# Second feed-forward product with the weights stationary and 448 tokens moving, its sums and the output transposed, the residual rebuilt on GpSimd

## The chip, the cores and the metric

The kernel runs on one core of a Trainium2 chip. The metric is the device time of one execution in microseconds (us). A core has TensorE (PE: matmuls; its weight loads are shown apart as PEld), VectorE (DVE), ScalarE (ACT), GpSimd (POOL) and SyncE (SP, which issues most of the DMAs). TensorE multiplies a stationary operand of 128 × 128 with a moving operand of up to 512 columns and adds the result up in PSUM, of which there are eight banks of 512 columns.

## What is computed

```python
x = attention(q, k, v)                 # 4 batches, 12 heads, 448 tokens, 64 each; causal softmax
x = x.transpose(0, 2, 1, 3).reshape(4, 448, 768)
gate = sigmoid(causal_conv5(x, conv_w))
x = (gate * (x @ w_val)) @ w_out       # 768 x 768 each
mu, var = mean(x), mean((x - mu) ** 2) # per token
xn = (x - mu) / sqrt(var + 1e-6) * g_ln
out = x + relu(xn @ w_ch1) @ w_ch2     # 768 -> 3072 -> 768; the kernel before sums x + ... in acc
```

## The kernel before

The kernel has three stages. The first does attention, convolution and gate, and the value product, batch by batch; its matmuls for the value product stand in line 517, and its output, feature by token, goes to DRAM (`y_dram`). The second, the norm stage, takes the 1,792 tokens as 14 tiles of 128: it loads a tile (`yl`, line 619), multiplies it with `w_out` (line 635, 36 matmuls of 384 columns), takes mean and variance from the result in PSUM, scales it (ScalarE, line 669), transposes it with six matmuls (line 677) and leaves the normed tile, feature by token, as a high and a low part (`xnh`, `xnl`). ScalarE also copies the sum itself to `acc[t]` (line 652), tokens in the partitions, as the residual.

The third stage is the feed-forward. Every float32 product is made of three matmuls: high × high, high × low, low × high. The 24 blocks of 128 hidden features are taken in 12 groups of two (`G = 2`), and the tokens in four steps of 256, 512, 512 and 512 (`TM`). For one group and step, `ch1` does the first product (`ch1_products`, line 586): the weights are stationary, the tokens move, and for each of the two blocks 18 matmuls are summed in one bank (six pieces of the 768 features times three parts). ScalarE applies relu and rounds (`hh`, line 747), VectorE makes the low part (`hl`, line 748). `ch2` does the second product (line 761): for each tile of 128 tokens `hh` and `hl` are stationary, and half a row of `w_ch2`, 384 columns, moves; six matmuls are summed, and VectorE adds the result to `acc[t]` (line 766). In the last group the finished tiles are stored.

The order of the third stage is written out: `ch1` runs two steps ahead of `ch2`, and behind each `ch2` some steps of the preparation of the next group's weights are issued (`advance`): VectorE turns the raw words of a block into float32 (lines 207 to 227), ScalarE rounds it (line 200), VectorE takes the low part (line 243). The order of the first two stages comes from a planner (`Plan`), which places tasks by due times and assumed costs. The first product of the first step, `ch1_products(0, 0, j)`, is one of its tasks and fills TensorE while the last tile is normed.

The outputs of the first product lie in three banks (`ps_1`) and, for the small step, in one (`ps_e`); those of the second in four (`ps_2`).

Of the kernel before, what the change touches and what calls it, by code (L numbers as in the profile page):

```python
# [145 lines left out]
def f32(ap):  # L146
    return ap.bitcast(F32)
# [3 lines left out]
def attention_gate_ffn(  # L151
# [12 lines left out]
    nc = tc.nc  # L164
    B, NP, P = qk.shape[:3]
    H, S = 2 * NP, out.shape[1]
# [10 lines left out]
    NEG_SCALE = -1.0 / float(D) ** 0.5  # L177
    ot = out.rearrange("b s d -> (b s) d")

# [11 lines left out]

    g_t = const.tile([P, KC], F32, name="g_t")
    y_dram = [dram.tile([DM, S], F32, name=f"y_dram{b}") for b in range(B)]

# [51 lines left out]
    with ExitStack() as ph1:  # L246
# [40 lines left out]
        task = plan.task  # L287
# [244 lines left out]

    accp = ctx.enter_context(tc.tile_pool(name="accp", bufs=1, reuse_waits="tile"))
    acc = [accp.tile([P, DM], F32, name=f"acc{t}") for t in range(NTILE)]
    G = 2
    TB = 4 * P
    TM = [list(range(NTILE % 4))] + [list(range(t, t + 4)) for t in range(NTILE % 4, NTILE, 4)]
    NM = len(TM)
    NG = NJ // G
    with ExitStack() as ph2:  # L540
        ff = ph2.enter_context(tc.tile_pool(name="ff", bufs=1, reuse_waits="tile"))
        xnh = ff.tile([P, KC, NT], F32R, name="xnh")
        xnl = ff.tile([P, KC, NT], F32R, name="xnl")
        w_t = {}

# [22 lines left out]

        ps_e = ph2.enter_context(tc.tile_pool(name="ps_e", bufs=1, space=PSUM))
        ps1_t = {}  # L570

        def ch1_products(g, m, j):
            lo, hi = TM[m][0] * P, (TM[m][-1] + 1) * P
            if m > 0:
                ps1_t[g, m, j] = ps_1.tile([P, 1, TB], F32, tag="a", name="ps1")
                ps = ps1_t[g, m, j][:, 0]
            else:
                if j == 0:
                    ps1_t[g] = ps_e.tile([P, G, hi - lo], F32, tag="e", name="ps1")
                ps1_t[g, m, j] = ps1_t[g]  # L580
                ps = ps1_t[g][:, j]
# [11 lines left out]
        with ExitStack() as ph2a, tc.manual_schedule():  # L593
# [6 lines left out]
                "yl": (yr_p, [P, KC, P], F32R, 3), "yh": (yr_p, [P, KC, P], F32R, 2),  # L600
                "st": (ln_p, [P, 2, 6], F32, 1), "mv": (ln_p, [P, 2], F32, 2), "rs": (ln_p, [P, 1], F32, 2),
                "nm": (ln_p, [P, 1], F32, 2), "xn": (ln_p, [P, DM], F32, 2), "o": (ps_a, [P, 2, 512], F32, 2), "x": (ps_x, [P, 8, P], F32, 1),
                "wraw": (wr, [P, DM, 2], U32, 1), "wt": (c2, [P, DM], F32, 2), "e": (ps_e, [P, G, TM[0][-1] * P + P], F32, 1),
            }, 0)
            task = plan.task
            o_last, x_of = None, {}

            def tile_steps(t):

                nonlocal o_last  # L610
                yl, yh, st, mv, rs, nm, xn, o, x = (Buf(k) for k in ("yl", "yh", "st", "mv", "rs", "nm", "xn", "o", "x"))

# [34 lines left out]
                def stats(e):  # L647
                    for nh in range(2):
                        nc.vector.bn_stats(st.tile[:, nh, :], o.tile[:, nh, :HALF])

                ks = task({"DVE": 930}, stats, t + 0.95, [k], [st], [o])
                ka = task({"ACT": 685}, lambda e: nc.scalar.copy(acc[t].rearrange("p (a f) -> p a f", a=2), o.tile[:, :, :HALF]),
                          t + 1.0, [k], [], [o])

                def moments(e):
                    nc.vector.bn_aggr(mv.tile, st.tile.rearrange("p a b -> p (a b)"))
                    nc.vector.tensor_scalar(rs.tile, mv.tile[:, 1:2], 1e-6, None, ALU.add)

                km = task({"DVE": 380}, moments, t + 1.05, [ks], [mv, rs], [st])

                def scale(e):
# [3 lines left out]
                km = task({"DVE": 150}, lambda e: nc.vector.scalar_tensor_tensor(  # L665
                    nm.tile, mv.tile[:, 0:1], -1.0, rs.tile, ALU.mult, ALU.mult), t + 0.9, [kr], [nm], [mv, rs])

# [58 lines left out]
            for j in range(G):  # L726
                task({"PE": 2200}, lambda e, j=j: ch1_products(0, 0, j), NTILE - 1 + 0.2 * (j + 1),
                     [first[j], o_last, *(x_of[t] for t in TM[0])])
            plan.run()

        with ExitStack() as ph2b, tc.manual_schedule():
            h_p = ph2b.enter_context(tc.tile_pool(name="h", bufs=2, reuse_waits="tile"))
            wb = ph2b.enter_context(tc.tile_pool(name="wb", bufs=1, reuse_waits="tile"))
            ps_1 = ph2b.enter_context(tc.tile_pool(name="ps_1", bufs=3, space=PSUM, reuse_waits="tile"))
            ps_2 = ph2b.enter_context(tc.tile_pool(name="ps_2", bufs=4, space=PSUM, reuse_waits="tile"))
            h_t = {}

            def ch1(g, m):
                hh = h_p.tile([P, G, TB], F32R, tag="hh", name="hh")[:, :, :len(TM[m]) * P]
                hl = h_p.tile([P, G, TB], F32R, tag="hl", name="hl")[:, :, :len(TM[m]) * P]  # L740
                parts = [(slice(j, j + 1), [j]) for j in range(G)] if m else [(slice(0, G), range(G))]
                for rows, js in parts:
                    for j in js:
                        if (g, m, j) not in ps1_t:
                            ch1_products(g, m, j)
                    ps = [ps1_t.pop((g, m, j)) for j in js][-1]
                    nc.scalar.activation(hh[:, rows], ps, AF.Relu)  # L747
                    nc.vector.scalar_tensor_tensor(hl[:, rows], ps, 0.0, f32(hh[:, rows]), ALU.max, ALU.subtract)  # L748
                h_t[g, m] = (hh, hl)

            def ch2(g, m):
                hh, hl = h_t.pop((g, m))
                for u, t in enumerate(TM[m]):
                    for nh in range(2):
                        half = slice(nh * HALF, (nh + 1) * HALF)
                        ps = ps_2.tile([P, 512], F32, tag="b", name="ps2")[:, :HALF]
                        n = 0
                        for j in range(G):
                            w = w_t[g, 1, j]
                            for x, a in ((hh, 0), (hh, 1), (hl, 0)):  # L760
# [3 lines left out]
                                n += 1  # L764
                        a = acc[t][:, half]
                        nc.vector.tensor_tensor(a, ps, a, ALU.add)  # L766
                        if g == NG - 1 and t == NTILE - 1:
                            nc.sync.dma_start(out=ot[t * P:(t + 1) * P, half], in_=a)
                    if g == NG - 1 and t < NTILE - 1:
                        nc.sync.dma_start(out=ot[t * P:(t + 1) * P, :], in_=acc[t])  # L770

            seq = [(g, m) for g in range(NG) for m in range(NM)]
            rest = keys[2 * G:]
            blocks = [w_steps(k, wb, (rest[n + 2], (wr, wb)[n % 2]) if n + 2 < len(rest) else None) for n, k in enumerate(rest)]
            load_block(rest[0], wr)
            load_block(rest[1], wb)

            taken = 0

            def advance(upto):  # L780
                nonlocal taken
                while taken < upto and blocks:
                    if next(blocks[0], 0) == 0:
                        blocks.pop(0)
                    else:
                        taken += 1

            PER = 7
            ahead = (9, 17, 21, 28)
            ch1(*seq[0])  # L790
            ch1(*seq[1])
            done = 2
            for i, (g, m) in enumerate(seq):
                ch2(g, m)
                advance(2 * PER * G * g + ahead[m])
                if m == NM - 1:
# [62 lines left out]
```

## Time and profile before

| | |
|---|---|
| median of 3 runs | 1056.14 us (1056.12 to 1056.38) |
| the profiled execution's own time | 1056.59 us |
| its span in the trace | 1054.8 us |
| busy share of the span | PE 99%, PEld 88%, DVE 67%, ACT 35%, POOL 18% |
| DMA | 83.59 MB in all, 79 GB/s in the mean |

The span is what the trace shows, from the first to the last instruction; the execution's own time lies 1.8 us above it. An engine's busy share is an average over three stages with different limits, so it says where to look and not what bounds a stage; and TensorE's matmuls overlap at their ends, so that its price per matmul is read from the distance between starts, or from the chain, and not from the duration of one.

### The profile page before, as it was taken

How to read it: one execution, taken by the hardware profiler on the slowest of the kernel's cores; microseconds unless marked ns; L12 is line 12 of the kernel's file. 1: busy time of each engine (PE TensorE's matmuls, PEld its weight loads, DVE VectorE, ACT ScalarE, POOL GpSimd, SP SyncE). 2: the span in 40 equal slices, each digit the busy share in tenths (PEclk: the TensorE clock that was granted, in tenths of full speed). 3: DMA queues.
4: the chain of work that ended last, by engine and by line, in shares of the span. 5: the costliest groups of instructions: out<-in, count | busy, mean ns of one | idle time of the engine just before them, and what ended most of it. 6: DMA issues, size and time to landing. Idle time of an engine off the chain costs nothing.

```text
span 1054.8 us, 15536 instructions
## 1 busy us (share of the span) xinstructions
PE 1041.7 (99%) x6163; PEld 926.3 (88%) x6163; DVE 708.5 (67%) x1341; ACT 365.2 (35%) x750; POOL 191.9 (18%) x277
## 2 busy tenths in 40 slices
PE   8889999999999999999999999999999999999998
PEld 5667777789999989998989999899989899998998
DVE  6888878773865376667666675766676666757633
ACT  7887878761554321112121121111121211211100
POOL 5889786680110000000000000000000000000000
PEclk9999999999999999999999999999999999999999
DMA  6344344332341011111110111111111101111023
GB/s 199 123 160 157 121 164 147 107 96 99 120 120 47 30 60 36 55 61 60 61 60 31 60 60 60 61 33 58 61 60 61 60 30 60 61 60 60 1 88 122
DMA packets 40983, 83.59 MB, mean 79 GB/s; under 512 B 5968, under 2 KB 29264, under 8 KB 40912
## 3 DMA queue, kind: packets, MB, share of 16 engines
q1 hardware_dynamic: 40768, 82.62, 23.3%
q8 instruction: 48, 0.79, 0.3%
q14 instruction: 23, 0.19, 0.1%
q10 hardware_dynamic: 144, 0.00, 0.0%
HBM read 71.60 MB, written 11.01 MB: 78 GB/s over the span
## 4 chain that ended last, share of the span: by engine, by line
PE 91%; DVE 4%; POOL 3%; ACT 2%; issue 0%; POOLq 0%; DVEq 0%
PE ps L761 33%; PE ps L586 32%; PE o L635 8%; PE val L517 5%; PE t L382 3%; PE pv L399 2%; PE s L517 2%; PE s L311 2%; POOL p L349 2%; DVE g L416 2%; PE s L314 1%; ACT p L340 1%; PE x L677 1%; DVE p L333 1%; PE pv L403 1%; POOL wvl L456 0%
## 5 line engine op out<-in xcount | busy, mean ns | idle before, releaser
L761 PE MATMUL ps<-wf,hh 128*128 128x384 f32 x1344 | 341.6, 335 | 0.0
L586 PE MATMUL ps<-xnh,wf 128*128 128x512 f32 (+1 forms) x1152 | 326.4, 363 | 0.0
L766 DVE TENSOR_TENSOR acc<-ps,acc 128x384 f32<-128x384 f32 x336 | 186.8, 556 | 128.5 <-PE ps L761 127.1
L761 PEld LDWEIGHTS ps<-wf,hh 128*128 128x128 f32 x1344 | 243.0, 188 | 2.8
L586 PEld LDWEIGHTS ps<-xnh,wf 128*128 128x128 f32 x1152 | 207.8, 189 | 33.0
L761 PE MATMUL ps<-wf,hl 128*128 128x384 f32 x672 | 225.0, 335 | 0.0
L586 PE MATMUL ps<-xnl,wf 128*128 128x512 f32 (+1 forms) x576 | 209.4, 364 | 0.0
L761 PEld LDWEIGHTS ps<-wf,hl 128*128 128x128 f32 x672 | 126.1, 188 | 0.0
L586 PEld LDWEIGHTS ps<-xnl,wf 128*128 128x128 f32 x576 | 108.6, 189 | 16.2
L200 ACT CAST wf<-w 128x768 fp32r<-128x768 f32 x44 | 36.7, 834 | 242.2 <-DVE w L227 137.9
L220 ACT ACTIVATE wraw<-wraw 128x768 f32<-128x768 f32 x60 | 55.1, 918 | 170.7 <-DVE w L209 169.7
L748 DVE SCALAR_TENSOR_TENSOR hl<-ps,hh 128x512 fp32r<-128x512 f32 x84 | 56.8, 687 | 68.8 <-ACT hh L747 68.8
L349 POOL TENSOR_SCALAR p<-p,r 128x128 f32<-128x128 f32 (+3 forms) x168 | 97.9, 603 | 26.5 <-DVE r L344 20.8
L747 ACT ACTIVATE hh<-ps 128x512 fp32r<-128x512 f32 x84 | 50.0, 596 | 142.8 <-PE ps L586 142.8
L340 ACT ACTIVATE p<-p,negm 128x128 f32<-128x128 f32 (+3 forms) x168 | 87.6, 525 | 10.5 <-DVE negm L333 10.2
L333 DVE CUSTOM_DVE_ANT_0 p<-s,mask 128x128 f32<-128x128 f32 (+3 forms) x168 | 66.4, 445 | 26.4 <-PE s L311 14.1
L243 DVE TENSOR_TENSOR wf<-w,wf 128x768 fp32r<-128x768 f32 x44 | 42.2, 959 | 39.6 <-ACT wf L200 39.6
L416 DVE SCALAR_TENSOR_TENSOR g<-pv,cw,g 128x444 f32<-128x444 f32 (+1 forms) x96 | 64.7, 673 | 3.7 <-POOL g L407 1.6
L635 PE MATMUL o<-wo,yh 128*128 128x384 f32 x336 | 62.5, 338 | 0.0
L382 PEld LDWEIGHTS t<-ident,p 128*128 128x128 f32 x384 | 43.7, 140 | 17.1 <-ACT pt L386 6.2
L635 PEld LDWEIGHTS o<-wo,yh 128*128 128x128 f32 x336 | 58.0, 188 | 0.0
L386 ACT COPY pt<-t 128x512 f32<-128x512 f32 x96 | 52.3, 584 | 15.8 <-PE t L382 15.6
(87 smaller groups left out, 1123.3 us busy)
## 6 DMA issues: line engine op xcount, KB each, us to landing
wraw<-in_w_ch SPq DMA_DIRECT2D x48, 768.0 KB, 4.3
raw<-in_qk SPq DMA_DIRECT2D x24, 512.0 KB, 3.9
v<-in_v SPq DMA_DIRECT2D x24, 256.0 KB, 3.0
y_dram<-g SPq DMA_DIRECT2D x24, 224.0 KB, 2.2
out<-acc SPq DMA_DIRECT2D x13, 384.0 KB, 2.3
wraw<-in_w_val SPq DMA_DIRECT2D x6, 768.0 KB, 5.0
wraw<-in_w_out SPq DMA_DIRECT2D x6, 768.0 KB, 4.4
yl<-y_dram SPq DMA_DIRECT2D x12, 384.0 KB, 3.5
```

What stands on the lines that cost most here:

```text
L220: nc.scalar.activation(f32(raw[:, :, 0]), f32(raw[:, :, 1]), AF.Abs)
L333: nc.vector.tensor_tensor_reduce(p.tile[:, o:o + w], src, m, NEG_SCALE, 3.0e38, ALU.add, ALU.min, negm.tile[:, i:i + 1])
L340: nc.scalar.activation(reg, reg, AF.Exp, bias=negm.tile[:, i:i + 1], scale=-1.0, accum_out=ssum.tile[:, i:i + 1])
L349: nc.gpsimd.tensor_scalar(reg, reg, r.tile[:, i:i + 1], 1.0, ALU.mult, ALU.mult)
L382: nc.tensor.transpose(bank.tile[:, j * P:(j + 1) * P], p.tile[:, o:o + P], ident)
L416: nc.vector.scalar_tensor_tensor(g.tile[:, d:], pv.tile[:, :S - d], cw[:, c, t:t + 1], g.tile[:, d:], ALU.mult, ALU.add)
L517: nc.tensor.matmul(ps.tile[:, :S], w[:, do, kc * P:(kc + 1) * P], x.tile, start=(kc == 0 and i == 0), stop=(kc == KC - 1 and i == 2),)
L586: nc.tensor.matmul(ps, wj[:, a, kc], x[:, kc, lo:hi], start=(n == 0), stop=(n == 3 * KC - 1))
L635: nc.tensor.matmul(o.tile[:, nh, :HALF], y.tile[:, kc], wo_t[kc][:, a, nh * HALF:(nh + 1) * HALF], start=(count[nh] == 0), stop=(count[nh] ...
L748: nc.vector.scalar_tensor_tensor(hl[:, rows], ps, 0.0, f32(hh[:, rows]), ALU.max, ALU.subtract)
L761: nc.tensor.matmul(ps, x[:, j, u * P:(u + 1) * P], w[:, a, half], start=(n == 0), stop=(n == 3 * G - 1))
L766: nc.vector.tensor_tensor(a, ps, a, ALU.add)
```

## The change

The second product is turned round. A piece of `w_ch2` of 128 × 128 is stationary, and the 448 tokens of one batch of `hh` or `hl` move; the result is 128 output features by 448 tokens. The four steps are now the four batches of 448 tokens, for the first product too. The sums (`acc[m][c]`) lie feature by token, and so does the output in DRAM; the host turns it round afterwards, outside the timed execution.

The residual can no longer be copied from the token-by-feature tile. It is rebuilt from the normed tile: x = (xnh + xnl) × deviation + mean. VectorE keeps the mean of each token in `md` and adds the deviation (a reciprocal, 14 times); ScalarE issues two DMAs that store both to DRAM; GpSimd loads them back as rows for all partitions (`row`) and does two additions and a product per piece of 128 features and batch, spread over the steps from the first group to the ninth. The first group's sums are copies.

PSUM: two banks for the even batches' first product (`ps_e`), two for the odd ones' (`ps_1`), four for the second product.

```diff
-        ps_e = ph2.enter_context(tc.tile_pool(name="ps_e", bufs=1, space=PSUM))
+        ps_e = ph2.enter_context(tc.tile_pool(name="ps_e", bufs=2, space=PSUM, reuse_waits="tile"))
...
         def ch1_products(g, m, j):
-            lo, hi = TM[m][0] * P, (TM[m][-1] + 1) * P
...
+            pool = ps_1 if m % 2 else ps_e
+            ps = ps1_t[g, m, j] = pool.tile([P, 512], F32, tag="e", name="ps1")[:, :S]
...
-                    nc.tensor.matmul(ps, wj[:, a, kc], x[:, kc, lo:hi], start=(n == 0), stop=(n == 3 * KC - 1))
+                    nc.tensor.matmul(ps, wj[:, a, kc], x[:, kc, m * S:(m + 1) * S], start=(n == 0), stop=(n == 3 * KC - 1))
...
-                ka = task({"ACT": 685}, lambda e: nc.scalar.copy(acc[t].rearrange("p (a f) -> p a f", a=2), o.tile[:, :, :HALF]),
-                          t + 1.0, [k], [], [o])
...
+                task({"DVE": 160}, lambda e: nc.vector.reciprocal(mv[:, 1:2], rs.tile), t + 1.3, [km], [], [rs])
...
+                for a in range(2):
+                    nc.scalar.dma_start(out=md_dram[a].rearrange("(t p) -> p t", p=P), in_=md[:, :, a])
...
+            def residual(m, i):
+
+                a = 1 if i < KC else 0
+                if i % KC == 0:
+                    row.append(rp.tile([P, S], F32, tag="row", name="row"))
+                    nc.gpsimd.dma_start(out=row[-1], in_=md_dram[a:a + 1, m * S:(m + 1) * S].to_broadcast([P, S]))
+                for c in [i] if a else range((i - KC) * 3, (i - KC) * 3 + 3):
+                    t = row[-1]
+                    if a:
+                        t = rp.tile([P, S], F32, tag="r", name="r")
+                        cols = slice(m * S, (m + 1) * S)
+                        nc.gpsimd.tensor_tensor(t, f32(xnh[:, c, cols]), f32(xnl[:, c, cols]), ALU.add)
+                        nc.gpsimd.tensor_tensor(t, t, row[-1], ALU.mult)
+                    nc.gpsimd.tensor_tensor(acc[m][c], t, acc[m][c], ALU.add)
...
             def ch2(g, m):
                 hh, hl = h_t.pop((g, m))
-                for u, t in enumerate(TM[m]):
-                    for nh in range(2):
...
-                                nc.tensor.matmul(
-                                    ps, x[:, j, u * P:(u + 1) * P], w[:, a, half], start=(n == 0), stop=(n == 3 * G - 1)
-                                )
...
+                for c in range(KC):
+                    ps = ps_2.tile([P, 512], F32, tag="b", name="ps2")[:, :S]
...
+                            nc.tensor.matmul(ps, w[:, a, c * P:(c + 1) * P], x[:, j], start=(n == 0), stop=(n == 3 * G - 1))
...
+                    a = acc[m][c]
+                    if g == 0:
+                        nc.vector.tensor_copy(a, ps)
+                    else:
+                        nc.vector.tensor_tensor(a, ps, a, ALU.add)
+                    if g == NG - 1:
+                        nc.sync.dma_start(out=out[m, c * P:(c + 1) * P, :], in_=a)
...
-            ahead = (9, 17, 21, 28)
+            ahead = (8, 15, 21, 28)
...
+                at = g * B + m - 3
+                if 0 <= at < B * (KC + 2):
+                    residual(*divmod(at, KC + 2))
```

How the instructions stand on the engines, at three places. A row is line, operation, output <- inputs and the shape written; x2 means that it stands twice.

TensorE at the end of one step's second product and the begin of another step's first, in the first group, before:

```order
L761 MATMUL ps_4218<-wf,hh 128x384 x2
L761 MATMUL ps_4218<-wf,hl 128x384
L586 MATMUL ps_4246<-xnh,wf 128x512
L586 MATMUL ps_4246<-xnl,wf 128x512
L586 MATMUL ps_4246<-xnh,wf 128x512 x2
```

and now:

```order
L774 MATMUL ps_4240<-hh,wf 128x448 x2
L774 MATMUL ps_4240<-hl,wf 128x448
L577 MATMUL ps_4267<-xnh,wf 128x448
L577 MATMUL ps_4267<-xnl,wf 128x448
L577 MATMUL ps_4267<-xnh,wf 128x448 x2
```

The moving operand stands ahead of the stationary one: in the second product the two have changed places, and both products have one width.

TensorE where the norm stage ends; the six transposes are those of the last tile, ahead of them stands the first product of the first step, behind them that of the second step. Before:

```order
L586 MATMUL ps_4059<-xnl,wf 128x256
L586 MATMUL ps_4059<-xnh,wf 128x256
L677 MATMUL x<-ident,xn 128x128 x6
L586 MATMUL ps_4152<-xnh,wf 128x512
L586 MATMUL ps_4152<-xnl,wf 128x512
```

and now:

```order
L577 MATMUL ps_4066<-xnl,wf 128x448
L577 MATMUL ps_4066<-xnh,wf 128x448
L669 MATMUL x<-ident,xn 128x128 x6
L577 MATMUL ps_4158<-xnh,wf 128x448
L577 MATMUL ps_4158<-xnl,wf 128x448
```

The order is the same; the 36 matmuls ahead of the last transposes have become wider.

ScalarE at the same place, before (the copies of the sum stand ahead of each norm `xn`):

```order
L652 COPY acc_3112<-o 128x768
L681 CAST xnh<-x 128x6x128
L200 CAST wf<-wt 128x768 x2
L669 ACTIVATE xn<-o,nm,rs 128x768
L681 CAST xnh<-x 128x6x128
L747 ACTIVATE hh<-ps_4059 128x2x256
```

and now:

```order
L673 CAST xnh<-x 128x6x128
L201 CAST wf<-wt 128x768
L736 DMA md_dram<-md 128x14x1
L661 ACTIVATE xn<-o,nm,rs 128x768
L736 DMA md_dram<-md 128x14x1
L745 ACTIVATE hh<-ps_4032 128x448
```

The copy is gone, and the two stores of mean and deviation stand ahead of and behind the last tile's norm.

## Rows read from the trace of the kernel before

**Rows 1.** The page: busy us, share and instructions; granted clock in 40 slices.

```profile
PE 1041.7 (99%) x6163; PEld 926.3 (88%) x6163; DVE 708.5 (67%) x1341; ACT 365.2 (35%) x750; POOL 191.9 (18%) x277
PEclk9999999999999999999999999999999999999999
```

**Rows 2.** Chain that ended last: start us, us, what; first group, last group's begin.

```profile
366.17 4.18 PE ps L761 x24
370.35 8.20 PE ps L586 x36
378.55 8.34 PE ps L761 x48
386.90 8.20 PE ps L586 x36
395.10 8.35 PE ps L761 x48
403.44 4.31 PE ps L586 x36
407.75 8.32 PE ps L761 x48
416.08 8.20 PE ps L586 x36
...
1005.41 4.18 PE ps L761 x24
```

**Rows 3.** The same chain: value product of the last batch, 448 columns.

```profile
234.74 21.89 PE s L517 x108
```

**Rows 4.** The same chain: where the norm stage ends.

```profile
345.20 0.65 PE x L677 x6
345.85 6.26 PE o L635 x36
...
353.20 0.80 ACT acc L652
...
354.70 1.47 ACT wf L200 x2
356.17 0.90 ACT xn L669
...
357.12 0.87 PE x L677 x6
357.99 8.18 PE ps L586 x36
```

**Rows 5.** Last sum (timeline); 448-column vector operation; DMA issues, KB each, us to landing.

```profile
1051.05 0.56 DVE L766 TENSOR_TENSOR acc<-ps,acc 128x384 f32<-128x384 f32 x1 [0.48 <-PE ps L761]
...
L527 DVE TENSOR_TENSOR g<-val,g 128x448 f32<-128x448 f32 x18 | 11.1, 619 | 5.8 <-PE val L517 5.4
...
out<-acc SPq DMA_DIRECT2D x2, 192.0 KB, 1.9
...
y_dram<-g SPq DMA_DIRECT2D x24, 224.0 KB, 2.2
```

**Rows 6.** Groups by shape: weight operation alone, beside GpSimd, two of them; GpSimd.

```profile
L223 DVE SCALAR_TENSOR_TENSOR w<-wraw,w 128x768 f32<-128x768 f32 x39 | 37.3, 956 | 3.0
...
L223 DVE SCALAR_TENSOR_TENSOR wt<-wraw,wt 128x768 f32<-128x768 f32 x16 | 16.4, 1023 | 0.1
...
96.71 1.36 DVE L223 SCALAR_TENSOR_TENSOR wt<-wraw,wt 128x768 f32<-128x768 f32 x1
...
638.26 0.96 DVE L243 TENSOR_TENSOR wf<-w,wf 128x768 fp32r<-128x768 f32 x1 [0.90 <-ACT wf L200]
...
L410 POOL TENSOR_TENSOR xl<-x,xh 128x448 fp32r<-128x448 f32 x24 | 28.6, 1194 | 2.0
```

**Rows 7.** Issue of y tile loads: durations ns min/median/max, first and last start.

```profile
L619 SPq DMA_DIRECT2D yl<-y_dram x13: 359/360/546, 262.9 to 331.4; - x13
```

More of the change, by code (lines that the diff above doesn't have):

```diff
@@ L165, in attention_gate_ffn @@
     B, NP, P = qk.shape[:3]
-    H, S = 2 * NP, out.shape[1]
+    H, S = 2 * NP, out.shape[2]
     D = P // 2
@@ L192, in attention_gate_ffn @@
     g_t = const.tile([P, KC], F32, name="g_t")
+    md_dram = dram.tile([2, NT], F32, name="md_dram")
     y_dram = [dram.tile([DM, S], F32, name=f"y_dram{b}") for b in range(B)]
@@ L531, in attention_gate_ffn @@
             plan.run()
-    accp = ctx.enter_context(tc.tile_pool(name="accp", bufs=1, reuse_waits="tile"))
-    acc = [accp.tile([P, DM], F32, name=f"acc{t}") for t in range(NTILE)]
     G = 2
-    TB = 4 * P
-    TM = [list(range(NTILE % 4))] + [list(range(t, t + 4)) for t in range(NTILE % 4, NTILE, 4)]
-    NM = len(TM)
     NG = NJ // G
@@ L543, in attention_gate_ffn @@
         xnl = ff.tile([P, KC, NT], F32R, name="xnl")
+        md = ff.tile([P, NTILE, 2], F32, name="md")
         w_t = {}
@@ L610, in tile_steps @@
                 nonlocal o_last
-                yl, yh, st, mv, rs, nm, xn, o, x = (Buf(k) for k in ("yl", "yh", "st", "mv", "rs", "nm", "xn", "o", "x"))
+                yl, yh, st, rs, nm, xn, o, x = (Buf(k) for k in ("yl", "yh", "st", "rs", "nm", "xn", "o", "x"))
+                mv = md[:, t]
                 def load(e):
@@ L651, in tile_steps @@
                 ks = task({"DVE": 930}, stats, t + 0.95, [k], [st], [o])
-                ka = task({"ACT": 685}, lambda e: nc.scalar.copy(acc[t].rearrange("p (a f) -> p a f", a=2), o.tile[:, :, :HALF]),
-                          t + 1.0, [k], [], [o])
                 def moments(e):
-                    nc.vector.bn_aggr(mv.tile, st.tile.rearrange("p a b -> p (a b)"))
-                    nc.vector.tensor_scalar(rs.tile, mv.tile[:, 1:2], 1e-6, None, ALU.add)
-                km = task({"DVE": 380}, moments, t + 1.05, [ks], [mv, rs], [st])
+                    nc.vector.bn_aggr(mv, st.tile.rearrange("p a b -> p (a b)"))
+                    nc.vector.tensor_scalar(rs.tile, mv[:, 1:2], 1e-6, None, ALU.add)
+                km = task({"DVE": 380}, moments, t + 1.05, [ks], [rs], [st])
                 def scale(e):
@@ L665, in tile_steps @@
                 km = task({"DVE": 150}, lambda e: nc.vector.scalar_tensor_tensor(
-                    nm.tile, mv.tile[:, 0:1], -1.0, rs.tile, ALU.mult, ALU.mult), t + 0.9, [kr], [nm], [mv, rs])
+                    nm.tile, mv[:, 0:1], -1.0, rs.tile, ALU.mult, ALU.mult), t + 0.9, [kr], [nm], [rs])
+                task({"DVE": 160}, lambda e: nc.vector.reciprocal(mv[:, 1:2], rs.tile), t + 1.3, [km], [], [rs])
                 def scaled(e):
@@ L726, in attention_gate_ffn @@
             for j in range(G):
-                task({"PE": 2200}, lambda e, j=j: ch1_products(0, 0, j), NTILE - 1 + 0.2 * (j + 1),
-                     [first[j], o_last, *(x_of[t] for t in TM[0])])
+                task({"PE": 3600}, lambda e, j=j: ch1_products(0, 0, j), NTILE - 1 + 0.2 * (j + 1),
+                     [first[j], o_last, *(x_of[t] for t in range(-(-S // P)))])
             plan.run()
         with ExitStack() as ph2b, tc.manual_schedule():
+            accp = ph2b.enter_context(tc.tile_pool(name="accp", bufs=1, reuse_waits="tile"))
@@ L732, in attention_gate_ffn @@
+            acc = [[accp.tile([P, S], F32, name=f"acc{m}_{c}") for c in range(KC)] for m in range(B)]
             h_p = ph2b.enter_context(tc.tile_pool(name="h", bufs=2, reuse_waits="tile"))
             wb = ph2b.enter_context(tc.tile_pool(name="wb", bufs=1, reuse_waits="tile"))
-            ps_1 = ph2b.enter_context(tc.tile_pool(name="ps_1", bufs=3, space=PSUM, reuse_waits="tile"))
+            rp = ph2b.enter_context(tc.tile_pool(name="rp", bufs=1, reuse_waits="tile"))
+            ps_1 = ph2b.enter_context(tc.tile_pool(name="ps_1", bufs=2, space=PSUM, reuse_waits="tile"))
@@ L735, in attention_gate_ffn @@
             ps_2 = ph2b.enter_context(tc.tile_pool(name="ps_2", bufs=4, space=PSUM, reuse_waits="tile"))
             h_t = {}
+            with nc.allow_non_contiguous_dma(reason="a mean and a deviation per token"):
+                for a in range(2):
+                    nc.scalar.dma_start(out=md_dram[a].rearrange("(t p) -> p t", p=P), in_=md[:, :, a])
             def ch1(g, m):
-                hh = h_p.tile([P, G, TB], F32R, tag="hh", name="hh")[:, :, :len(TM[m]) * P]
-                hl = h_p.tile([P, G, TB], F32R, tag="hl", name="hl")[:, :, :len(TM[m]) * P]
@@ L741, in ch1 @@
[L741 to L748, printed above, removed]
@@ L749, in ch1 @@
-                h_t[g, m] = (hh, hl)
+                hh = h_p.tile([P, G, S], F32R, tag="hh", name="hh")
+                hl = h_p.tile([P, G, S], F32R, tag="hl", name="hl")
+                for j in range(G):
+                    if (g, m, j) not in ps1_t:
+                        ch1_products(g, m, j)
+                    ps = ps1_t.pop((g, m, j))
+                    nc.scalar.activation(hh[:, j], ps, AF.Relu)
+                    nc.vector.scalar_tensor_tensor(hl[:, j], ps, 0.0, f32(hh[:, j]), ALU.max, ALU.subtract)
@@ L751, in ch2 @@
+            row = []
             def ch2(g, m):
                 hh, hl = h_t.pop((g, m))
-                for u, t in enumerate(TM[m]):
-                    for nh in range(2):
[L755 to L760, printed above, removed]
-                                nc.tensor.matmul(
-                                    ps, x[:, j, u * P:(u + 1) * P], w[:, a, half], start=(n == 0), stop=(n == 3 * G - 1)
-                                )
-                                n += 1
-                        a = acc[t][:, half]
-                        nc.vector.tensor_tensor(a, ps, a, ALU.add)
[L767 to L770, printed above, removed]
@@ L772, in attention_gate_ffn @@
-            seq = [(g, m) for g in range(NG) for m in range(NM)]
+                for c in range(KC):
+                    ps = ps_2.tile([P, 512], F32, tag="b", name="ps2")[:, :S]
+                    n = 0
+                    for j in range(G):
+                        w = w_t[g, 1, j]
+                        for x, a in ((hh, 0), (hh, 1), (hl, 0)):
+                            nc.tensor.matmul(ps, w[:, a, c * P:(c + 1) * P], x[:, j], start=(n == 0), stop=(n == 3 * G - 1))
+                            n += 1
+                    a = acc[m][c]
+                    if g == 0:
+                        nc.vector.tensor_copy(a, ps)
+                    else:
+                        nc.vector.tensor_tensor(a, ps, a, ALU.add)
+                    if g == NG - 1:
+                        nc.sync.dma_start(out=out[m, c * P:(c + 1) * P, :], in_=a)
@@ L773, in attention_gate_ffn @@
+            seq = [(g, m) for g in range(NG) for m in range(B)]
             rest = keys[2 * G:]
```

19 lines of the change are left out of this document (5 added, 14 removed).

## The prediction

> **What bounds the kernel now.** I read the page first: TensorE is busy for 99% of the span, and the granted clock is full, its 2.4 GHz level, in all forty slices [rows 1]. A busy TensorE says little by itself, so I read the chain of work that ended last, in order of time. From 366 us to the last output it is nothing but matmuls of the two feed-forward products, one piece of 36, 24 or 48 behind the other, with no other engine in between [rows 2]. What the reader is to see there is the price of one matmul by its width: 36 of 512 columns take 8.20 us (227.8 ns each), 48 of 384 columns 8.35 us (173.9 ns), 36 of 256 columns 4.31 us (119.7 ns). One group of two weight blocks takes (1005.41 − 366.17) / 11 = 58.11 us, and there are twelve. So in this stretch the change is worth what it does to the sum of matmul prices, plus whatever makes TensorE wait.
>
> Before that stretch the chain runs through the norm stage [rows 4], and at its very end through one vector sum and one store [rows 5].
>
> **The change, part by part.**
>
> *The two products.* All matmuls become 448 columns wide. Per group the first product keeps 4 × 36 = 144 matmuls, now of one width in place of 36 × 256 and 108 × 512; the second goes from 24 + 3 × 48 = 168 of 384 columns to 4 × 6 × 6 = 144 of 448. The columns streamed are the same in both (64,512 each), so the only question is what one 448-column matmul costs. The kernel before has such matmuls, in the value product of the gate stage: same operand type, 128 × 128 stationary, 18 summed into one bank, the same order of high and low parts. In the last batch they stand back to back, and the chain has 108 of them in 21.89 us: 202.7 ns each [rows 3]. That is more than the half-way point between 384 and 512 columns, (173.9 + 227.8) / 2 = 200.8 ns. I take 202.7, because it is a measurement of the width itself, made while no other engine held TensorE up; and because width alone seems to set the price: the output projection of the norm stage, another layout with another operand stationary, pays 6.26 / 36 = 173.9 ns for its 384 columns [rows 4], as the second product does.
>
> A group then takes 288 × 21.89 / 108 = 58.37 us, against 58.11: +0.26 us, and 12 × 0.26 = **+3.1 us**. Split by product: the first goes from 3 × 8.20 + 4.31 = 28.91 to 144 × 0.2027 = 29.19 us; the second from 4.18 + 8.34 + 8.35 + 8.32 = 29.19 [rows 2] to the same 29.19. The 24 matmuls that it saves per group are paid back in full by their width.
>
> *The end of the norm stage.* Now TensorE leaves the last projection tile at 352.11, transposes tile 12, does the first product of the small first step, and then needs the last normed tile, which ScalarE finishes at 357.07 after a copy of the sum (0.80), two weight casts (1.47) and other work [rows 4]. From 352.11 to 357.99 it spends 5.88 us on work worth 4.31 + 2 × 0.65 = 5.61. With 448 columns the first step lasts 7.3 us, and the copy is gone, so the tile is ready long before: **−0.3 us** (at most the whole 0.27, at least nothing). The fourteen copies that go and the fourteen reciprocals that come (one number per token) lie beside TensorE's projection in the same stage, which the chain shows without a gap; nothing for either.
>
> *The two stores of mean and deviation*, issued by ScalarE, one of them ahead of the last norm. No row shows a store of single numbers. The nearest issue is the load of a y tile: 768 rows, 0.36 us of the queue [rows 7]; 1,792 numbers in proportion are 0.84 us, an estimate. TensorE comes to the last transposes at 352.11 + 0.65 + 7.3 = 360.1, and ScalarE had their input ready at 357.07 before, so it may be held about 3 us longer for nothing; the second store has until the second product begins, 7 us later. I take 0; what lies beyond 3 us is paid once.
>
> *The residual on GpSimd.* 96 additions and products of 448 columns, at 1.19 us each (the nearest row) 114 us in all, three per step of 14.6 us [rows 6]. Each piece may run once VectorE has left the tile, and VectorE wants it back one group, 58 us, later; so no sum waits for it, nor for the row that GpSimd's queue loads. What it can do is slow VectorE. In a step VectorE ends its last sum 0.7 us after the second product, does at most seven weight operations of 0.96 and waits 0.90 for a cast [rows 6], then two low parts of 0.62 each (the price of a 448-column operation with one operand in PSUM [rows 5]): it comes to the next sums at 0.7 + 6.7 + 0.9 + 1.2 = 9.5 us and frees the first buffer at 10.1. TensorE, with 7.3 us of first product and four buffers of 1.22, wants it at 12.2. That leaves 2.1 us. With GpSimd busy beside it the widest of these operations took 1023 ns in the mean in place of 956, and 1.36 us at worst [rows 6]: six times 0.07 is 0.4 us, well inside. I take 0; bounds 0 and +10 us (below).
>
> *The end.* The last sum has 448 columns in place of 384, 0.62 for 0.56, and the last store 224 KB for 192, 2.2 for 1.9 us [rows 5]: **+0.4 us** at most, 0.1 at least.
>
> The sum: 3.1 − 0.3 + 0.4 = +3.2 us, on the profiled execution's own 1056.59 us (span 1054.8, 1.8 around it): 1059.8. The median of the runs lies 0.45 us under that execution, so I give **1059.3 us**. A measurement of this kernel can tell about 0.2%, 2.1 us, from no change.
>
> **The rivals.**
>
> *One line through all widths (faster).* 256, 384 and 512 columns lie on one line, 54 ns per 128 columns with a fixed part of 12 ns, and 448 may lie on it in these two products: 200.8 ns. A group is then 288 × 0.2008 = 57.82 us, 12 × −0.29 = −3.5, and with the two ends −3.4: 1052.7 on the scale of the median. For it: three widths agree, and the 448-column rows come from another stage, with each operand in a tile of its own. Against it: those 108 rows are long, even and undisturbed, and the 384-column price did not change between stages. It decides from about 201.8 ns downwards, where a group breaks even. The Trainium skill ("TensorE: Matmul & The Clock Gate", Back-to-back issue gap) has such a line, N/2.4 + 2.5 ns; by it the change would save 288 × 2.5 ns = 0.7 us, and every row here lies above it (202.7 against 189.2 for 448 columns).
>
> *Half and half (no change).* Only one of the products pays 202.7, for instance because the second has other neighbours in its banks. By the split above a group then takes 58.09 to 58.13 us, the ends all but cancel, and the time is 1055.5 to 1057.
>
> *GpSimd holds VectorE, VectorE holds TensorE (much slower).* If every one of six weight operations of a step took the worst row, +0.40 each, VectorE would be 2.4 us late against 2.1 of slack; 0.3 us in each of 32 steps is +10: 1069. It decides above 0.35 us per operation; the mean in the rows is 0.07. The Trainium skill ("SBUF — State Buffer", SBUF: two separate sides) says that a vector operation with two inputs in SBUF and a GpSimd operation exclude each other for the whole instruction. Three full GpSimd instructions of 1.19 us per step would be 3.6 us, 1.5 over the slack and 1107 in the end; the rows of the gate stage, where both engines are busy, show far less.
>
> **Chances.** Forecast 0.60, its own range 1058.3 to 1060.5; one line 0.25; half and half 0.08; GpSimd 0.07. The range 1052.2 to 1061.5 holds the forecast, half and half and most of the second. Faster 0.25; within 0.2% 0.11 (half and half, and the forecast's lower edge); slower 0.64.
>
> **What would show it.** In the chain after, 36-matmul pieces of 7.3 us and a group of 58.4 us mean that I am right; 7.2 and 57.8 or less mean the first rival. At 352 us no gap of TensorE ahead of the last transposes. Waits of a matmul for VectorE in the feed-forward part would mean the last rival; weight operations there should grow by less than 0.1 us. I am wrong if 448 columns cost something else in this stage than in the gate stage.

## The result, and the profile after

The changed kernel takes 1066.61 us (1066.05 to 1067.05, five runs) against 1056.16 for the kernel before (five runs): ratio 1.0097 (95% interval 1.0083 to 1.0112), 10.45 us slower. I had said 1059.3, with a range up to 1061.5. The sign was right, the size was not: 3.2 us were foreseen and 10.5 came.

The page of the changed kernel, against [rows 1]: TensorE is as full as before and its clock is still at the 2.4 GHz level in all slices. GpSimd, which stood still after the first third, now works in bursts (its line of tenths).

```profile
PE 1049.4 (99%) x5875; PEld 929.8 (87%) x5875; DVE 732.6 (69%) x1319; ACT 359.1 (34%) x748; POOL 330.9 (31%) x381
...
POOL 6889786670100020602505044050440500000000
PEclk9999999999999999999999999999999999999999
```

The chain of work that ended last, against [rows 2] and [rows 4]: the end of the norm stage, then two stretches of the feed-forward part (start us, us, what).

```profile
345.80 6.25 PE o L627 x36
...
352.71 7.35 PE ps L577 x36
...
360.72 7.34 PE ps L577 x36
368.06 7.36 PE ps L774 x36
...
427.33 7.34 PE ps L774 x36
...
435.92 1.80 DVE w L210
...
437.75 1.81 DVE w L212
...
448.15 2.72 PE ps L774 x12
450.87 7.29 PE ps L577 x36
```

Two things are new. First, the pieces of 36 matmuls do not last 7.30 us, as [rows 3] price them, but mostly 7.33 to 7.34; some first products keep 7.29 to 7.31. Over 96 pieces that is some 3 us. Second, the chain leaves TensorE (here it is on VectorE at 435.92): VectorE's preparation of a weight block takes so long that the second product waits for a free buffer. The piece that begins at about 442 us lasts 8.9 us in place of 7.34. There are four such places, from 376, 436, 774 and 833 us on, worth 0.5, 1.6, 0.8 and 0.7 us by the starts of the matmuls. Three more pieces, at 405, 575 and 877 us, last 7.42 to 7.43.

The weight operations there are twice as long as in [rows 6]. Beside them stands GpSimd. The timeline of both in that stretch (start us, us, engine, operation, idle before):

```profile
435.24 0.64 DVE L208 TENSOR_SCALAR w<-wraw 128x768 uint32<-128x768 uint32 x1
435.92 1.79 DVE L210 SCALAR_TENSOR_TENSOR w<-wraw,w 128x768 uint32<-128x768 uint32 x1
437.75 1.80 DVE L212 SCALAR_TENSOR_TENSOR w<-wraw,w 128x768 uint32<-128x768 uint32 x1
...
434.31 1.15 POOL L762 TENSOR_TENSOR acc<-r,acc 128x448 f32<-128x448 f32 x1
435.55 1.35 POOL L760 TENSOR_TENSOR r<-xnh,xnl 128x448 f32<-128x448 f32 x1
436.98 1.76 POOL L761 TENSOR_TENSOR r<-r,row 128x448 f32<-128x448 f32 x1
438.81 1.74 POOL L762 TENSOR_TENSOR acc<-r,acc 128x448 f32<-128x448 f32 x1
```

Both engines pay: 0.96 becomes 1.80 and 1.16 becomes 1.75. And GpSimd runs its pieces one behind the other. In the program they stand one per step, but a piece waits for nothing of its step: only for the last sum of its own tile, which comes once in four steps. So four pieces, twelve operations, run in a row here, from 430.6 to 448.7 us, long enough to cover the whole preparation of a block.

### The profile page after: what moved, and what is told of

Same layout as the page of the kernel before. It is cut to its first block, busy times and chain, and to the rows that moved or that the text cites. A ratio compares the mean times of both kernels' runs of the same rounds, so it can differ in the third digit from the quotient of the medians.

```text
span 1064.3 us, 15138 instructions
## 1 busy us (share of the span) xinstructions
PE 1049.4 (99%) x5875; PEld 929.8 (87%) x5875; DVE 732.6 (69%) x1319; ACT 359.1 (34%) x748; POOL 330.9 (31%) x381
## 4 chain that ended last, share of the span: by engine, by line
PE 88%; DVE 8%; POOL 3%; ACT 1%; issue 1%; DVEq 0%; POOLq 0%
PE ps L774 32%; PE ps L577 30%; PE o L627 8%; PE val L518 5%; PE t L383 3%; PE pv L400 2%; PE s L312 2%; PE s L518 2%; POOL p L350 2%; DVE g L417 2%; PE s L315 1%; DVE p L334 1%; PE x L669 1%; PE pv L404 1%; DVE w L212 1%; DVE w L210 1%
## 5 line engine op out<-in xcount | busy, mean ns | idle before, releaser
L577 PE MATMUL ps<-xnh,wf 128*128 128x448 f32 x1152 | 335.8, 366 | 0.0
L774 PE MATMUL ps<-hh,wf 128*128 128x448 f32 x1152 | 328.9, 366 | 2.4 <-DVE acc L780 1.3
L780 DVE TENSOR_TENSOR acc<-ps,acc 128x448 f32<-128x448 f32 x264 | 163.4, 623 | 122.1 <-PE ps L774 121.1
L774 PEld LDWEIGHTS ps<-hh,wf 128*128 128x128 f32 x1152 | 216.1, 188 | 22.5 <-DVE acc L780 1.9
L774 PE MATMUL ps<-hl,wf 128*128 128x448 f32 x576 | 210.6, 366 | 0.0
L577 PE MATMUL ps<-xnl,wf 128*128 128x448 f32 x576 | 210.6, 366 | 0.0
L774 PEld LDWEIGHTS ps<-hl,wf 128*128 128x128 f32 x576 | 108.2, 188 | 9.1
L762 POOL TENSOR_TENSOR acc<-r,acc 128x448 f32<-128x448 f32 x24 | 34.3, 1429 | 237.8 <-DVE acc L780 189.6
L746 DVE SCALAR_TENSOR_TENSOR hl<-ps,hh 128x448 fp32r<-128x448 f32 x96 | 58.1, 619 | 52.9 <-ACT hh L745 52.7
L745 ACT ACTIVATE hh<-ps 128x448 fp32r<-128x448 f32 x96 | 51.2, 542 | 91.6 <-PE ps L577 91.5
```

Of the source, the lines that this page charges most:

```text
L577: nc.tensor.matmul(ps, wj[:, a, kc], x[:, kc, m * S:(m + 1) * S], start=(n == 0), stop=(n == 3 * KC - 1))
L746: nc.vector.scalar_tensor_tensor(hl[:, j], ps, 0.0, f32(hh[:, j]), ALU.max, ALU.subtract)
L762: nc.gpsimd.tensor_tensor(acc[m][c], t, acc[m][c], ALU.add)
L774: nc.tensor.matmul(ps, w[:, a, c * P:(c + 1) * P], x[:, j], start=(n == 0), stop=(n == 3 * G - 1))
```

## The experiments

**Without GpSimd's residual.**

```diff
-                at = g * B + m - 3
-                if 0 <= at < B * (KC + 2):
-                    residual(*divmod(at, KC + 2))
```

> The changed kernel without the residual's 96 GpSimd operations and row loads; the output lacks x. Theory (GpSimd's residual runs in bursts, beside them VectorE's weight operations take 1.8 us in place of 0.96, and TensorE waits for VectorE at four places): the four waits vanish, 0.5 + 1.6 + 0.8 + 0.7 = 3.6 us less, 1063.0 us; every weight operation at 0.96; the price of a 448-column matmul stays at 203.0 to 203.9 ns, so the kernel stays slower than before by some 6.9 us. Rival (VectorE is late by the new order of its work alone, the wider sums and the new amounts of weight preparation per step): 1066.6, the waits stay. Second rival (GpSimd also raises the price of TensorE's matmuls): pieces fall to 7.30 us and the time to about 1059.5.

Measured: 1061.93 us (1061.40 to 1062.44). The waits are gone, and the weight operations are back where [rows 6] have them. Groups in the feed-forward part (count, busy us, mean ns, idle before), the changed kernel first:

```profile
L780 DVE TENSOR_TENSOR acc<-ps,acc 128x448 f32<-128x448 f32 x264 | 163.4, 623 | 122.1 <-PE ps L774 121.1 <-issue 0.2
...
L224 DVE SCALAR_TENSOR_TENSOR w<-wraw,w 128x768 f32<-128x768 f32 x44 | 50.3, 1143 | 4.8 <-ACT wraw L221 0.3
```

and without the residual:

```profile
L780 DVE TENSOR_TENSOR acc<-ps,acc 128x448 f32<-128x448 f32 x264 | 164.7, 624 | 132.9 <-PE ps L774 132.3
...
L224 DVE SCALAR_TENSOR_TENSOR w<-wraw,w 128x768 f32<-128x768 f32 x44 | 42.2, 958 | 4.8 <-ACT wraw L221 0.3
```

Over the five kinds of weight operation that grew, VectorE loses 29 us to GpSimd, and the whole kernel 4.7 by the medians: the rest lay in VectorE's slack. Of the 4.7 the two chains show 3.8 from the first full step to the last matmul, which is the four waits and the three pieces of 7.42 to 7.43. The remainder lies ahead of it, where runs with the same instructions differ: the first product begins anywhere from 351.8 to 352.9 us. The sums, with one operand in PSUM, do not grow. The second rival falls: the pieces stay at 7.31 to 7.34 us with an idle GpSimd, so the higher price is not GpSimd's doing. Of the excess, 5.8 us remain.

**The residual paced.** The same 96 operations; a row is loaded for each piece, each step now takes the piece whose sum comes first in that step, and the order of the six sums turns with the group.

```diff
+                first = (0, 0, 1, 2, 3, 4, 5, 0, 3, 0, 0, 0)[g]
-                for c in range(KC):
+                for c in [*range(first, KC), *range(first)]:
...
-                if 0 <= at < B * (KC + 2):
-                    residual(*divmod(at, KC + 2))
+                if 1 <= g <= KC + 2:
+                    residual(m, g - 1)
```

> The changed kernel with the same residual work, one piece per step, on the tile whose sum comes first in that step's second product, so that GpSimd works while VectorE does sums (one operand in PSUM) and is idle while VectorE prepares weights. A row is loaded for each piece. Theory (it is the overlap of GpSimd with the weight operations that costs, not GpSimd's work as such): no matmul waits for VectorE, as without the residual, 1063.0 us (1062.6 to 1064). Rival (GpSimd's work slows VectorE wherever it stands, so that sums too take longer than 0.62 us): at least half of the 3.6 us stays, 1065 or more.

Measured: 1062.31 us (1062.22 to 1062.56), 4.3 less than the changed kernel, and 0.4 more in the median than without any residual (I had expected 1062.6 at least). GpSimd's operations take 1.15 to 1.18 us and the weight operations 0.96 to 0.98 in the mean: it was the place, not the work.

**GpSimd operations with one input,** in the bursts as they were.

```diff
-                        nc.gpsimd.tensor_tensor(t, f32(xnh[:, c, cols]), f32(xnl[:, c, cols]), ALU.add)
-                        nc.gpsimd.tensor_tensor(t, t, row[-1], ALU.mult)
-                    nc.gpsimd.tensor_tensor(acc[m][c], t, acc[m][c], ALU.add)
+                        nc.gpsimd.tensor_scalar(t, f32(xnh[:, c, cols]), 1.0, 1.0, ALU.mult, ALU.mult)
+                        nc.gpsimd.tensor_scalar(t, t, 1.0, 1.0, ALU.mult, ALU.mult)
+                    nc.gpsimd.tensor_scalar(acc[m][c], acc[m][c], 1.0, 1.0, ALU.mult, ALU.mult)
```

> The changed kernel with each of GpSimd's residual operations put in the form of a product of one tensor with a constant (one SBUF input in place of two); number, place, bursts and row loads stay, the output lacks x. Theory A (VectorE is held up only by GpSimd operations with two SBUF inputs): weight operations at 0.96 throughout, no wait, 1063.0 us. Theory B (any GpSimd operation of this size holds them up): weight operations that lie beside GpSimd at up to 1.8 us, and 1064.5 to 1066.6, by how long the new operations last.

Measured: 1062.77 us (1061.77 to 1063.08). Neither theory as it stood. The timeline of the same stretch:

```profile
435.67 1.19 DVE L210 SCALAR_TENSOR_TENSOR w<-wraw,w 128x768 uint32<-128x768 uint32 x1
436.89 1.20 DVE L212 SCALAR_TENSOR_TENSOR w<-wraw,w 128x768 uint32<-128x768 uint32 x1
...
434.00 0.57 POOL L760 TENSOR_SCALAR r<-xnh 128x448 f32<-128x448 f32 x1
...
436.02 1.26 POOL L760 TENSOR_SCALAR r<-xnh 128x448 f32<-128x448 f32 x1
437.36 1.15 POOL L761 TENSOR_SCALAR r<-r 128x448 f32<-128x448 f32 x1
```

One input still holds VectorE up, but by 0.24 us in place of 0.84, and GpSimd itself goes from 0.57 to 1.15. As the bursts are also half as long, almost nothing reaches TensorE.

**Other token steps in the new layout.** Steps of 256, 512, 512 and 512 as before, `w_ch2` stationary, the residual in paced pieces of 256 tokens.

```diff
+    TM = [(max(0, 512 * m - 256), 512 * m + 256) for m in range(NT // 512 + 1)]
...
+            lo, hi = TM[m]
-                    nc.tensor.matmul(ps, wj[:, a, kc], x[:, kc, m * S:(m + 1) * S], start=(n == 0), stop=(n == 3 * KC - 1))
+                    nc.tensor.matmul(ps, wj[:, a, kc], x[:, kc, lo:hi], start=(n == 0), stop=(n == 3 * KC - 1))
```

> The new layout (weights stationary in the second product, sums and output feature by token) with the token steps of the kernel before, 256 and three times 512, and the residual in pieces of 256 tokens, paced as in the paced run. Theory (the price of a matmul goes by its width alone, 119.7 ns for 256 and 227.8 for 512 columns, and 448 is a dear width): the second product of a group takes 3 x 8.20 + 4.31 = 28.91 us in place of 29.19, a group 57.82 in place of 58.11, 12 x 0.29 = 3.5 less; norm stage 0.3 less, end up to 0.5 more: 1052.9 us (1052 to 1054), faster than both kernels. Rival (it is the new layout that is dear, about 1 ns per matmul in the second product whatever its width): 1054.6 or more. Rival (the residual still holds VectorE up in steps of 256 tokens): matmuls wait for VectorE, 1056 or more.

Measured: 1062.35 us (1061.85 to 1062.90). My theory of the width fell here, by far. The chain:

```profile
436.47 8.39 PE ps L780 x36
444.86 8.17 PE ps L579 x36
...
474.11 8.39 PE ps L579 x36
482.50 4.32 PE ps L780 x36
486.82 8.36 PE ps L579 x36
```

The second product (L780) always pays 8.36 to 8.40 us for 36 matmuls of 512 columns. The first product (L579) pays 8.17 to 8.21 in one group and 8.36 to 8.40 in the next, with the same instructions. What differs from group to group is the place of its weights: in every other group they lie in two buffers of their own (`wq`). So it is not 448 columns alone, and in the first product, whose layout the change leaves as it was, not the new layout.

**Narrower columns, and hidden values apart.** Three runs stream 384, 416 or 320 of the 448 tokens; another lets each row of hidden values begin at a multiple of 512 numbers. All without the residual.

```diff
-                    nc.tensor.matmul(ps, wj[:, a, kc], x[:, kc, m * S:(m + 1) * S], start=(n == 0), stop=(n == 3 * KC - 1))
+                    nc.tensor.matmul(ps, wj[:, a, kc], x[:, kc, m * S:m * S + 384], start=(n == 0), stop=(n == 3 * KC - 1))
...
-                hh = h_p.tile([P, G, S], F32R, tag="hh", name="hh")
+                hh = h_p.tile([P, G, 512], F32R, tag="hh", name="hh")[:, :, :S]
```

> As without the residual, and both products stream only the first 384 of the 448 tokens of each batch (64 tokens of each batch and the residual are left out). Theory (width): 173.9 ns per matmul as 384 columns cost elsewhere, pieces of 6.26 us. Rival (the layout is dear): 175 ns or more, 6.30 or more.

> As the run with 384 tokens, with 416 of 448. The line through 256, 384 and 512 columns gives 187.4 ns, pieces of 6.75 us. Theory (widths that are no multiple of 128 lie above the line): 189 ns or more, 6.80 or more. Rival (448 alone lies off it): 187.4.

> As the run with 384 tokens, with 320 of 448. The line gives 146.8 ns, pieces of 5.28 us. Theory (widths that are no multiple of 128 lie above the line): 149 ns or more, 5.36 or more. Rival (448 alone lies off it): 146.8. VectorE has less time per step here, so waits for it may appear; the price is read from pieces without one.

> As without the residual (output lacks x), and each row of 448 hidden values in hh and hl now begins at a multiple of 512 numbers, so that the moving operand of the second product begins at another place in SBUF; nothing else changes. Theory (the price goes by the width): pieces of the second product stay at 7.33 to 7.34 us. Rival (it goes by where the moving operand begins): they fall to 7.30 (the price of the gate stage) or to 7.23 (one line through the other widths), the first product's pieces stay.

Measured, one run each: 964.17, 1010.27, 872.30 and 1061.26 us. With 320 columns a piece takes 5.27 to 5.29 us where nothing waits, in both products: 146.6 ns, on the line. With 416 there are pieces of 6.72, 6.79 and 6.83 to 6.84 us, without one rule that I could see. With the hidden values apart nothing changes (7.31 and 7.34). That says less than I meant it to: 512 numbers in place of 448 move the second row by 256 bytes and every tile behind by a multiple of it, a move that costs nothing in the runs below either. The run with 384 columns shows the pattern again, 6.34 us in the second product, and in the first 6.34 in one group, 6.24 in the next:

```profile
586.50 6.34 PE ps L577 x36
592.84 6.34 PE ps L777 x36
599.18 6.24 PE ps L577 x36
```

So I looked up where the operands lie (bytes in a partition, from the built programs):

```
                        kernel before          changed kernel
normed tile (xnh)       103104   (192)         60096   (192)
weights, most blocks     17088   (192)         17088   (192)
weights in wq           189120   (192)        146240    (64)
hidden values (hh)      201408   (192)        201536    (64)
in brackets: modulo 256
```

In the kernel before both operands of each of these matmuls begin at the same place modulo 256. The same holds for the value product (both operands at 128) and the output projection (both at 192). The change puts a tile of 112 bytes (`md`), which takes up 128, ahead of `wq` and the hidden values, and the pair is 128 bytes apart in all of the second product and in every other group of the first: just the dear ones at 384, 448 and 512 columns. With 416 columns it does not come out so: the second product, 128 bytes apart throughout, takes 6.72 us in some pieces and 6.83 to 6.84 in others.

**The small tile made 256 bytes long,** in the paced kernel and in the one with steps of 256 and 512.

```diff
-        md = ff.tile([P, NTILE, 2], F32, name="md")
+        md = ff.tile([P, 64], F32, name="md")[:, :2 * NTILE].rearrange("p (t a) -> p t a", a=2)
```

> The paced run with the tile of mean and deviation, 112 bytes per partition, made 256 bytes long, so that every tile behind it (two of the weight blocks and the hidden values) begins 128 bytes later; instructions and order are the same. Theory (a matmul is dearer when its moving and its stationary operand begin 128 bytes apart, counted modulo 256; in the kernel before they never do, in the changed kernel they do in all of the second product and in every other group of the first): 448 columns at 203.0 ns in both products, 1728 x 0.85 + 864 x 0.66 ns = 2.0 us less than the paced run, 1060.3 us. Rival (the price hangs on the layout or on which weight block is used, not on the address): 1062.3, pieces as they were.

> The run with token steps of 256 and three times 512 in the new layout, with the same tile made 256 bytes long. Theory (address): 512 columns at 227.8 ns in place of 232.9 in all of the second product and half of the first, 256 columns at 119.5 to 119.9: 1296 x 5.1 + 648 x 5.1 ns = 9.9 us, and 0.1 more for the small steps, less than 1062.35: 1052.3 us (1051.5 to 1053.5), faster than the kernel before. Rival (layout or block): 1062.3.

Measured: 1058.86 us (1058.70 to 1059.34, ratio to before 1.0027, 1.0016 to 1.0037), 3.45 less; and 1050.28 us (1049.99 to 1050.71, ratio 0.9946, 0.9934 to 0.9958), 12.1 less. Both gain more than expected (2.0 and 10.0). Of the 3.45 the chains show 3.1 from the first full step to the last matmul, the rest ahead of it. The chain of the first, where every piece now has the price of [rows 3]:

```profile
360.12 7.30 PE ps L577 x36
...
382.01 7.30 PE ps L774 x36
389.31 7.30 PE ps L577 x36
...
418.49 7.30 PE ps L577 x36
```

and of the second, with 8.16 to 8.19 us for 36 matmuls of 512 columns in both products, a little under the 8.20 of [rows 2]:

```profile
426.99 8.19 PE ps L579 x36
435.18 8.16 PE ps L780 x36
443.34 8.16 PE ps L579 x36
```

That is a version faster than both kernels; it beats the kernel before by 5.8 us (0.5%).

**The kernel before, with its hidden values moved.** An unused tile ahead of them, of 128, 256 or 64 bytes.

```diff
+            apart_p = ph2b.enter_context(tc.tile_pool(name="apart", bufs=1, reuse_waits="tile"))
+            nc.gpsimd.memset(apart_p.tile([P, 32], F32, name="apart"), 0.0)
             h_p = ph2b.enter_context(tc.tile_pool(name="h", bufs=2, reuse_waits="tile"))
```

> The kernel before with an unused tile of 128 bytes per partition ahead of the hidden values, which then begin 128 bytes later; one memset more on an idle GpSimd, nothing else. Theory (address): the second product's 384-column matmuls, hidden values stationary, rise from 173.9 to 176.1 ns, 2016 x 2.2 = 4.4 us more, 1060.6 us (to 1061.7 if they rise by 2.75); the first product keeps its pieces of 8.20 us. Rival: 1056.2, no change.

> The same with 256 bytes. Theory (it is the distance modulo 256 that counts): 1056.2 us, as the kernel before, 173.9 ns. Rival (any move of the hidden values costs): about 1060.6, as with 128 bytes.

> The kernel before with the hidden values 64 bytes later, as the run with 128 bytes. If all that is no multiple of 256 costs alike, 1060.4 us and 176.1 ns for 384 columns; if only the 128-byte half counts, 1056.2 us and 173.9 ns; if it costs by the distance, some 1058.

Measured: 1060.40 us (ratio 1.0044, 1.0032 to 1.0057), 1056.42 (1.0003, 0.9994 to 1.0012) and 1057.10 (1.0012, 1.0004 to 1.0021). The chains, in the order 128, 256, 64 bytes; the second product is L763, here with the hidden values stationary:

```profile
619.89 8.21 PE ps L586 x36
628.10 8.46 PE ps L763 x48
```

```profile
619.29 8.20 PE ps L586 x36
627.50 8.34 PE ps L763 x48
```

```profile
619.76 8.18 PE ps L586 x36
627.94 8.38 PE ps L763 x48
```

One unused tile of 128 bytes costs the kernel before 4.3 us, and one of 256 nothing. 64 bytes cost about 1 us: neither nothing nor the whole. Nor is 64 bytes dear everywhere: in the changed kernel the output projection has its operands 64 bytes apart (192 and 0, as here; from the built programs), and its 36 matmuls of 384 columns still take 6.25 us, against 6.26 in [rows 4].

**The 256 bytes alone,** in the changed kernel with its bursts (the diff of `md` above).

> The changed kernel with the tile of mean and deviation made 256 bytes long and nothing else changed; GpSimd's bursts stay. If the two causes are independent, it loses what the paced run lost, 3.45 us, and takes 1063.2 us (1062.6 to 1063.8), with four waits for VectorE of the same length. If a faster TensorE only comes sooner to the same late VectorE, the waits grow: 4 x 0.15 us or more of the gain is lost, 1063.8 or more.

Measured: 1066.25 us in the median, but from 1063.11 to 1068.34 over six runs. Two runs lie at 1063.1, where two independent causes would put it, four at 1066.06 or more. The profile is of one of these four (1066.06). Its chain at the last wait for VectorE:

```profile
814.79 7.29 PE ps L577 x36
822.09 7.31 PE ps L774 x36
...
830.59 1.81 DVE w L210
...
837.97 6.88 PE ps L774 x32
844.84 7.44 PE ps L577 x36
852.28 7.44 PE ps L774 x36
```

Up to 830 us every undisturbed piece lasts 7.29 to 7.31 us. Behind the last wait TensorE has another even pace, 206.7 ns per matmul, and keeps it to the end: 29 pieces, 29 × 0.14 = 4.1 us, at full granted clock and with no wait in the chain. The waits themselves hardly grew (8.9, 8.1 and 8.2 us for the three longest pieces, by the starts of the matmuls, against 8.9, 8.1 and 8.0), and the first of the four is gone. So both of my cases missed what happened. The new pace begins with the last wait, but that the wait set it off is not shown: the two waits ahead of it left the pace as it was. That the other three of the four had the same is likely, not shown; what picks the pace is open.

## Why the prediction was wrong

In the order in which the causes were taken away, the medians give 4.3 us for GpSimd's bursts (1066.61 to 1062.31), 3.45 for the 128 bytes (to 1058.86) and 2.8 for the rest (to 1056.09, the kernel before in that round), 10.5 together. By the chains of the feed-forward part the first two are 3.8 and 3.1. The last run says that this split holds for this order; with the bursts left in, the bytes alone gave their gain in two runs of six.

*The two products, +3.1.* The price from [rows 3], 202.7 ns, was right for operands that lie alike: when both disturbances are gone a group takes 58.37 us (360.12 to 418.49 above), just as forecast, and what is left, 2.8 us, is near the sum that I had made for products and ends (3.2). The step that failed is "width alone seems to set the price". Every row of the kernel before that I compared has its operands alike modulo 256, so that no row could show the other case; the new tile in the diff, and what lies behind it, I did not follow. Missing term: +3.45.

*The residual on GpSimd, "I take 0".* This is the other step that failed. The slack of 2.1 us per step was about right (at 774 us three operations are 2.5 us longer together, and TensorE loses 0.8). The price was not: I took 0.07 us per operation, a mean over a stage in which GpSimd seldom stands beside these operations, and called 0.40 the worst; side by side it is 0.84. And I spread the pieces over the steps as the program does, though nothing holds GpSimd to its step. The rival had the mechanism, at a chance of 0.07, but with a small loss in each of 32 steps; it came as four large ones. Missing term: +4.3.

The Trainium skill ("SBUF — State Buffer", SBUF: two separate sides) says that a vector operation with two inputs in SBUF and a GpSimd operation that reads SBUF lock each other out for a whole instruction. The trace agrees in that the sums with an operand in PSUM stay at 0.62 us, and in that a GpSimd operation with one input holds VectorE up too (1.20); but 1.80 and 1.75 us side by side are less than the 0.96 + 1.16 = 2.12 that strict turns would take. The 1107 us that I worked out from the rule was far off, because it let the two meet in every step.

*The rivals on the other side.* One line through all widths did not come at 448 columns: 7.30 us at best, not 7.23. At 320 columns it holds (146.6 ns).

*The end of the norm stage, −0.3.* Right: the chain has no ScalarE ahead of the last transposes any more, and the first full step begins at 360.72 behind a product of 7.35 and six transposes. *The end, +0.4 at most.* The last sum takes 0.62 us (timeline), the store 1.9 us for 224 KB and not 2.2 (DMA issues):

```profile
1060.78 0.62 DVE L780 TENSOR_TENSOR acc<-ps,acc 128x448 f32<-128x448 f32 x1 [0.59 <-PE ps L774]
```

```profile
out<-acc SPq DMA_DIRECT2D x24, 224.0 KB, 1.9
```

From the begin of the last sum to the end of the span it is 3.5 us (1060.78 to 1064.3), against 3.75 before (1051.05 in [rows 5] to 1054.8): 0.2 less, and not 0.1 to 0.4 more.

*The two stores.* Each landed after 13.9 us and GpSimd's first load waited for it; nothing on the chain did.

## What to carry to other kernels

A new tile moves everything behind it: where TensorE is the bound, look up where the moving and the stationary operand of the costliest matmuls begin modulo 256, before and after, and pad what shifts them (at 384, 448 and 512 columns this case shows a price for it). Work put on an idle engine should be tied to the stretch in which its neighbour does something that doesn't collide; program order does not hold it there, only a wait does. And a price read from a trace holds for the conditions of its rows, so ask which of them the change alters, the addresses too.

## What the runs showed of the hardware that was not expected

- The price of a matmul (fp32r, 128 × 128 stationary) with operands alike modulo 256 and 128 bytes apart, from pieces of 36 or 48: 384 columns 173.3 to 173.9 ns against 175.8 to 176.2; 448 columns 202.5 to 203.1 against 203.6 to 203.9; 512 columns 226.7 to 228.1 against 232.2 to 233.3; at 320 columns no difference (146.6). So the surcharge does not grow evenly with the width: 2 to 3, 1 and 5 ns.
- It does not matter which of the two has moved: in the kernel before the stationary side went, in the changed one the moving side (second product) and the stationary one (`wq`), and with 384 columns each of these costs 2 to 3 ns. Not told apart is whether it is the distance or the place of the moved operand itself: in every dear run that one begins at 64 modulo 256 and the other at 192, and no run has both at 64.
- TensorE has more than one steady pace for the same 448-column matmuls at full clock, 202.7 and 206.7 ns; one trace shows the second, from a wait on to the end of the kernel.
- A vector operation with two SBUF inputs goes from 0.96 to 1.80 us beside GpSimd operations with two, and to 1.20 beside those with one; GpSimd's go from 1.16 to 1.75 and from 0.57 to 1.15.
